# Seven half products for eight in part of the first FFN product, with copies moved to GpSimd: an attention and FFN kernel on one core

## The chip, the core and the metric

One core of a Trainium2 chip. Its engines are TensorE (PE: matmuls, and PEld: the weight loads beside them), VectorE (DVE), ScalarE (ACT), GpSimd (POOL) and SyncE (SP), each with its own queue of instructions, tied together by semaphores. The metric is the time of one execution on the device in microseconds (us); less is better.

## The reference

Eight batches of local and global attention (8 heads of 64, 512 local and 32 global tokens, a window of 32 tokens to either side), and then an FFN with a gelu over all 4352 tokens:

```python
s_g = scale * q_g @ k_all.T;  out_g = softmax(s_g) @ v_all        # 32 global queries see all
s_l = [scale * q_l @ k_g.T, scale * q_l @ k_l.T inside |i - j| <= 32]
out_l = softmax(s_l) @ [v_g, v_l]
x = concat(out_g, out_l) as (tokens, 512)
h = x @ w_in                     # (tokens, 512) x (512, 2048): the first FFN product
g = h * (1 / (1 + exp(-1.702 * h)))
out = g @ w_out                  # (tokens, 2048) x (2048, 512): the second
```

Inputs and output are float32; the kernel multiplies in bf16 and sums in float32.

## The kernel before, in words

The order of all instructions is written out by hand (`tc.manual_schedule()`): each engine gets its instructions in the order of the Python statements, and the Tile layer adds the semaphore waits and rotates the buffers of each pool.

The attention works on `Quad`s (four heads of one batch), two per batch, called `a` and `c`, each in its wide form `Wide`. Keys and queries are loaded by DMAs on POOL's queue (`load`, L81 and L82; `v` in `load_v`, L98 and L100), turned by transposes on DVE (`Tk`, L512; `Tq`, L316), and rearranged by small copies: `kcopy` (L504, 192 float32 a partition), `qcopy` (L507, 384 bf16) and the four parts of `ext` (L538, L540, L543, L545: the columns of the global queries and keys). `S` makes scores (L560), `X` the exponentials on ACT (L571), `M` multiplies them by the mask (L576, on DVE, and once per batch on POOL), `U` and `Gm` the products with `v` (L586, L597), `R` the reciprocal of the sums, with two transposes on DVE through the tiles `sT` and `rs` (L462 to L466), and `XL` the result (L471), which is the batch's `xL`, [128, 4, 512] in bf16: 512 channels in four blocks, 512 tokens.

The first FFN product of a batch is 16 calls of `h_step(i, fc)`: four matmuls of 512 columns (L615, one for each block of channels) into a PSUM bank `hp`, then one gelu on ACT (L620) into block `fc` of `gT`. Blocks are paired: pair `g` is the blocks 2g and 2g+1. The four `pbank` banks (`hp`, `ov`, `px` and others) rotate; the pairs of double banks from `spair` hold scores.

The second FFN product of batches 2 to 7 and of the 256 global rows (called batch 8) is written as seven half products for eight (`Pair`, L701 on): sums of quarters of `gT` (`g_sums`, on DVE, L696 and L699, in calls over groups of pairs), sums of the weights made once (`weight_sums`), seven products `mm(1)` to `mm(7)` of 256 columns (L726) into the banks `px` and `py`, and the combining steps `m3` (ACT), `z`, `zm`, `sub`, `add` (DVE) and `evict` (ACT) into `zz` and `ob`, which goes out by DMAs on SP's queue.

For batch i from 2 on the program alternates. First come the 16 steps of the first product, between which stand the transposes and copies of the next batch's `c` and of the batch after next's `a` (called `a2`), and the `g_sums` of the blocks that are ready:

```python
for fc in range(FC):
    h_step(i, fc)
    ...
    if i + 1 < B:
        c = nq[i + 1][1]
        if fc == 1:
            c.Tk(); c.Tq(); c.ext((3,))
        if fc in (3, 5, 7):
            c.ext(((3, 5, 7).index(fc),), on_act)
        if fc == 9 and i + 2 < B:
            a2 = quads_of(i + 2)[0]
            a2.T(); transpose_g(2 * i + 4, 2 * i + 6); a2.ext()
    if fc in (4, 8, 12):
        g_sums(i, fc // 2 - 2, fc // 2)
```

Then `phase_o(i)` interleaves the two `Pair`s of the second product, `p0` and `p1`, with the attention of batch i + 1, and at its end issues the loads of later batches (`loads_after`). After batch 7 the steps of the 256 global rows stand between the products of batch 7.

Of the kernel before, what the change touches and what calls it, by code (L numbers as in the profile page):

```python
# [12 lines left out]
F32 = mybir.dt.float32  # L13
# [3 lines left out]
ALU = mybir.AluOpType  # L17
# [3 lines left out]
def kernel(  # L21
# [90 lines left out]
    def on_act(out_, in_):  # L112
        nc.scalar.activation(out_, in_, AF.Copy)  # L113
# [166 lines left out]
    def pbank(name):  # L280
        return psP.tile([128, 512], F32, name=name, tag="p")


    def spair():
        return [psS.tile([128, 2, 512], F32, name="s4", tag="s%d" % i) for i in range(2)]
# [4 lines left out]
    class Quad:  # L290
        def __init__(self, Q):
            self.Q = Q
            self.b, self.u = divmod(Q, 2)
            if self.u == 0:
                xL[self.b] = att.tile([128, NKC, Sl], BF16, name="xL", bufs=2)
            self.x = xL[self.b]
            self.v = v_view(self.b, 5 if self.b else 4)[:, self.u]
            self.qt = qtiles[Q % 4]
            self.q = self.qt.bitcast(BF16).rearrange("p t (r e) -> p t r e", e=2)
            self.qg = qgT[:, Q, :32].bitcast(BF16).rearrange("p (s e) -> p s e", e=2)  # L300
            self.kg = kgT[:, Q].bitcast(BF16).rearrange("p (s e) -> p s e", e=2)
            self.E = [None, None]
            self.bk = {}
            self.st = {}
            self.pt = None
            self.gr = 1
# [297 lines left out]
            self.Gm()  # L604

    gTs, ops = {}, {}

    def width(i):
        return TB if i < B else B * Sg
# [3 lines left out]
    def h_mm(i, fc, hp, kcs):  # L613
        for kc in kcs:
            nc.tensor.matmul(hp[:, : width(i)], lhsT=w_in_c[:, fc // 4, kc, fc % 4 // 2, :, fc % 2],  # L615
                             rhs=(xL[i] if i < B else xG)[:, kc, :],
                             start=(kc == 0), stop=(kc == NKC - 1))

    def gelu(out_, in_):
        nc.scalar.activation(out_, in_, AF.Gelu_apprx_sigmoid)  # L620
# [15 lines left out]
    def h_act(i, fc, hp):  # L636
        n = width(i)
        gelu(gTs[i][:, fc, :n], hp[:, :n])

    def h_step(i, fc):  # L640
        if fc == 0:
            gTs[i] = (moe.tile([128, FC, TB], BF16, name="gT") if i < B else
                      early.bitcast(BF16).rearrange("p a b -> p (a b)").rearrange("p (f t) -> p f t", f=FC))
        hp = pbank("hp")
        h_mm(i, fc, hp, range(NKC))
        h_act(i, fc, hp)

    def o_mm(i, st, out=True, part=range(4)):
        tci, f4 = divmod(st, 4)
        first = (i, tci) not in ops  # L650
        if first:
            ops[i, tci] = pbank("op")
        op = ops[i, tci]
        for fc in [4 * f4 + n for n in part]:
            nc.tensor.matmul(op, lhsT=gTs[i][:, fc, tci * 128 : tci * 128 + 128],  # L655
                             rhs=w_out_sb[:, fc, :], start=(first and fc == 4 * f4), stop=(fc == FC - 1))
        if f4 == 3 and 3 in part and out:
            o_out(i, tci, op)

    HT = TB // 2  # L660
    HM = d_model // 2
    w_out_c = w_out_sb.rearrange("p (g e) m -> p g e m", e=2)
    b11, b12, b21, b22 = (w_out_c[:, :, e, h * HM : h * HM + HM] for e in range(2) for h in range(2))
    wsum = [wts.tile([128, FC // 2, HM], BF16, name="wsum%d" % k) if k in (0, 3, 4) else (b12, b21)[k - 1]
# [36 lines left out]
    class Pair:  # L701
# [5 lines left out]
        def mm(self, *ks):  # L707
            i, tt = self.i, self.tt
            n = width(i) // 2
            a11, a12, a21, a22 = parts_of(i)  # L710
            s = sums[i]
            for k in ks:
                lv, rv, where = {
                    1: (s[0], wsum[0], 2), 2: (s[2][:, :, n : 2 * n], b11, 1), 3: (a11, wsum[1], 0),
                    4: (a22, wsum[2], 1), 5: (s[2], b22, 0), 6: (s[1], wsum[3], 3), 7: (s[3], wsum[4], 2),
                }[k]
                if self.apart:
                    out_ = self.banks[where][:, :HM]
                else:
                    if k == 3:  # L720
                        self.x = self.banks[0] if self.banks else pbank("px")
                    if k == 1:
                        self.y = self.banks[1] if self.banks else pbank("py")
                    out_ = (self.y if where > 1 else self.x)[:, where % 2 * HM : where % 2 * HM + HM]
                for g in range(FC // 2):
                    nc.tensor.matmul(out_, lhsT=lv[:, g, tt * 128 : tt * 128 + 128], rhs=rv[:, g, :],  # L726
                                     start=(g == 0 and k in ((1, 3, 4, 6) if self.apart else (1, 3))), stop=(g == FC // 2 - 1 and k in (2, 5, 6, 7)),
                                     skip_group_check=True)

        def m3(self, eng="act"):  # L730
            self.zz = moe.tile([128, 2, HM], F32, name="zz")
            if eng == "act":
                on_act(self.zz[:, 0], self.x[:, :HM])
            else:
                nc.vector.tensor_copy(self.zz[:, 0], self.x[:, :HM])

        def z(self):
            nc.vector.tensor_add(self.zz[:, 0], self.zz[:, 0], self.x[:, HM:])

        def zm(self):  # L740
            nc.vector.tensor_add(self.zz[:, 1], self.zz[:, 0], self.y[:, :HM])
# [5 lines left out]
        def sub(self):  # L747
            nc.vector.tensor_sub(self.zz, self.zz, self.x.rearrange("p (h m) -> p h m", h=2))  # L748

        def add(self):  # L750
            nc.vector.tensor_add(self.ob[:, 0:4:3], self.zz, self.y.rearrange("p (h m) -> p h m", h=2))
# [104 lines left out]
    c.G()  # L856
    for fc in range(4, FC):
        h_step(0, fc)
    def osteps(i, *sts):
        for tci, f4 in sts:  # L860
            o_mm(i, 4 * tci + f4)
# [105 lines left out]
    def quads_of(n):  # L967
        if n < B and n not in nq:
            nq[n] = (Wide(2 * n), Wide(2 * n + 1))
        return nq.get(n, (None, None))  # L970
# [44 lines left out]
    def phase_o(i):  # L1015
        b = i + 1
        a, c = nq[b]
        a2, c2 = quads_of(b + 1)
        p0, p1 = Pair(i, 0), Pair(i, 1)
        exp_table()  # L1020
        a.UG()
        c.S(0)
        a.R()
        g_sums(i, 7, 8, (0,))
        a.XL(0)
        g_sums(i, 7, 8, (1, 2))
        a.XL(1)
        g_sums(i, 7, 8, (3,))
        p0.mm(3, 4, 1)
        c.X(0)  # L1030
        p0.m3()
        p0.z()
        a.G()
        c.M(0)
        c.S(1)
        c.X(1)
        p0.mm(6)
        p0.zm()
        c.M(1)
        p0.mm(5, 2)  # L1040
        p0.sub()
        p0.evict()
        p0.mm(7)
        p0.add()
        p0.store()
        if a2:
            c.UG()
            c.R()
            a2.S(0)
            a2.X(0)  # L1050
            a2.M(0, nc.gpsimd)
            loads_after(i + 1)
        else:
            pt = spair()
            c.U(0, bank(pt, 0))
            c.U(1, bank(pt, 2))
            c.U(2, bank(pt, 3))
            c.Gm(bank(pt, 1))
            c.R()
        c.XL(0)  # L1060
        if a2:
            c.XL(1)
            c.G()
        p1.mm(3, 4)
        p1.m3()
        p1.z()
        if not a2:
            c.XL(1)
            c.G()
        p1.mm(1, 6)  # L1070
        p1.zm()
        if a2:
            a2.S(1)
            a2.X(1)
        p1.mm(5, 2)
        p1.sub()
        p1.evict()
        gelu_table()
        p1.mm(7)
        p1.add()  # L1080
        if a2:
            a2.M(1)
        p1.store()

    for i in range(1, B):
        if i > 1:
            for fc in range(FC):
                h_step(i, fc)
                if i == 2 and fc == 0:
                    weight_sums(1, 2)  # L1090
# [3 lines that stand above are left out]
                        c.Tk()  # L1094
                        c.Tq()
                        c.ext((3,))
# [4 lines that stand above are left out]
                        a2.T()  # L1101
                        transpose_g(2 * i + 4, 2 * i + 6)
                        a2.ext()
                if fc in (4, 8, 12):
                    g_sums(i, fc // 2 - 2, fc // 2)
                if fc == 13:
                    g_sums(i, 6, 7)
        if i == 1:
            phase_o1()
        elif i + 1 < B:  # L1110
            phase_o(i)
# [88 lines left out]
```

## Time and profile before

| what | value |
|---|---|
| time, median of 3 runs | 286.68 us (286.36 to 286.75) |
| the profiled execution's own time | 286.51 us |
| its span in the trace | 284.5 us |
| PE busy | 279.1 us, 98% of the span, 3727 matmuls |
| DVE busy | 205.2 us, 72%, 498 instructions |
| ACT busy | 183.7 us, 65%, 293 |
| POOL busy | 95.2 us, 33%, 142 |
| granted TensorE clock | 1.0 |

PE's busy share alone does not say that PE is the limit, because matmuls overlap each other in the records; the chain of waits and the starts of successive matmuls do. The durations below are those of the one profiled execution. Times in the timelines count from the start of the span, and 2.0 us of the execution's own time lie outside it.

### The profile page before, as it was taken

How to read it: one execution, taken by the hardware profiler on the slowest of the kernel's cores; microseconds unless marked ns; L12 is line 12 of the kernel's file. 1: busy time of each engine (PE TensorE's matmuls, PEld its weight loads, DVE VectorE, ACT ScalarE, POOL GpSimd, SP SyncE). 2: the span in 40 equal slices, each digit the busy share in tenths (PEclk: the TensorE clock that was granted, in tenths of full speed). 3: DMA queues.
4: the chain of work that ended last, by engine and by line, in shares of the span. 5: the costliest groups of instructions: out<-in, count | busy, mean ns of one | idle time of the engine just before them, and what ended most of it. 6: DMA issues, size and time to landing. Idle time of an engine off the chain costs nothing.

```text
span 284.5 us, 8846 instructions
## 1 busy us (share of the span) xinstructions
PE 279.1 (98%) x3727; PEld 179.6 (63%) x3727; DVE 205.2 (72%) x498; ACT 183.7 (65%) x293; POOL 95.2 (33%) x142
## 2 busy tenths in 40 slices
PE   8999999999999999999999999999999999999994
PEld 7554445444554488647884588547874588448884
DVE  7670378995689998679957997779867697363452
ACT  4857568567778783878468764877568760873331
POOL 8974551857855002930077003900040000000001
PEclk9999999999999999999999999999999999999999
DMA  7999996999999702792039803970022003200213
GB/s 207 156 196 210 204 155 93 155 215 143 171 192 143 146 2 68 81 194 52 22 65 160 149 3 78 93 73 5 20 67 66 2 2 77 74 0 2 74 38 113
DMA packets 59351, 28.23 MB, mean 99 GB/s; under 512 B 47472, under 2 KB 49776, under 8 KB 59312
## 3 DMA queue, kind: packets, MB, share of 16 engines
q0 software_dynamic: 51760, 17.83, 55.3%
q1 hardware_dynamic: 7120, 9.18, 11.7%
q8 instruction: 29, 0.48, 0.7%
q10 hardware_dynamic: 432, 0.66, 0.7%
q14 instruction: 10, 0.08, 0.1%
HBM read 36.31 MB, written 8.91 MB: 159 GB/s over the span
## 4 chain that ended last, share of the span: by engine, by line
PE 94%; DVE 2%; DMA 1%; ACT 1%; SPq 0%; issue 0%; DVEq 0%
PE hp L615 38%; PE px L726 13%; PE op L655 10%; PE py L726 9%; PE x L726 6%; PE s L560 6%; PE ov L586 5%; PE s L615 3%; DMA early<-in_q_l_dram 1%; DVE xL L471 1%; PE og L597 1%; PE s L357 1%; ACT e L388 1%; PE ov L438 1%; PE s L340 1%; ACT e L385 0%
## 5 line engine op out<-in xcount | busy, mean ns | idle before, releaser
L615 PE MATMUL hp<-xL,w_in_sb 128*128 128x512 bf16 x480 | 105.4, 379 | 0.2 <-DVE xL L471 0.2
L615 PEld LDWEIGHTS <-w_in_sb 128*128 128x128 bf16 x576 | 56.1, 98 | 60.1 <-issue 0.4
L620 ACT ACTIVATE gT<-hp 128x512 bf16<-128x512 f32 x120 | 70.0, 596 | 25.1 <-PE hp L615 23.6
L571 ACT ACTIVATE e<-s 128x1016 bf16<-128x1016 f32 (+1 forms) x56 | 53.3, 1003 | 24.0 <-PE s L560 24.0
L726 PEld LDWEIGHTS <-gs 128*128 128x128 bf16 x480 | 46.3, 98 | 6.4
L699 DVE TENSOR_TENSOR gs<-gT 128x512 bf16<-128x512 bf16 (+1 forms) x90 | 30.3, 363 | 17.5 <-ACT gT L620 17.3
L576 POOL TENSOR_TENSOR e<-e,mask 128x1760 bf16<-128x1760 bf16 x4 | 13.3, 3320 | 83.4 <-ACT e L571 83.4
L98 POOL DMA_DIRECT2D v<-in_v_l_dram x40 | 31.1, 780 | 13.7 <-PE og L597 4.4
L726 PE MATMUL py<-wsum,gs 128*128 128x256 bf16 x240 | 30.3, 273 | 0.0
L655 PE MATMUL op<-w_out_sb,gT 128*128 128x512 bf16 x128 | 29.5, 380 | 0.0
L576 DVE TENSOR_TENSOR e<-e,mask 128x1712 bf16<-128x1712 bf16 (+1 forms) x24 | 25.1, 1048 | 3.7 <-ACT e L571 3.7
L512 DVE STREAM_TRANSPOSE kT<-rk 128x512 f32<-128x512 f32 x14 | 14.6, 1042 | 16.8 <-DMA rk<-in_k_l_dram 16.8
L759 POOL DMA_DIRECT2D out_dram<-ob x2 | 1.2, 597 | 68.2 <-ACT ob L113 68.0
L655 PEld LDWEIGHTS <-gT 128*128 128x128 bf16 x128 | 11.8, 98 | 14.0
L726 PEld LDWEIGHTS <-gT 128*128 128x128 bf16 x192 | 18.0, 98 | 2.9
L726 PE MATMUL px<-w_out_sb,gT 128*128 128x256 bf16 x160 | 19.2, 273 | 0.0
L726 PE MATMUL px<-w_out_sb,gs 128*128 128x256 bf16 x160 | 19.1, 273 | 0.0
L471 DVE TENSOR_TENSOR xL<-ov,rs 128x512 bf16<-128x512 f32 x27 | 17.9, 685 | 1.1 <-DVE rs L466 0.5
L696 DVE TENSOR_TENSOR gs<-gT 128x1024 bf16<-128x1024 bf16 (+1 forms) x30 | 17.3, 577 | 0.0
L560 PEld LDWEIGHTS <-kT 32*128 32x128 bf16 x672 | 12.5, 93 | 6.9 <-issue 4.9
L113 ACT ACTIVATE ob<-px 128x512 f32<-128x512 f32 x10 | 6.0, 599 | 15.2 <-DVE zz L748 15.2
L560 PE MATMUL s<-q,kT 32*128 32x160 bf16 (+1 forms) x448 | 14.7, 246 | 0.0
(153 smaller groups left out, 361.5 us busy)
## 6 DMA issues: line engine op xcount, KB each, us to landing
out_dram<-ob SPq DMA_DIRECT2D x128, 64.0 KB, 2.1
rq<-in_q_l_dram POOLq DMA_DIRECT2D x5, 512.0 KB, 8.5
rk<-in_k_l_dram POOLq DMA_DIRECT2D x5, 512.0 KB, 10.4
v<-in_v_l_dram POOLq DMA_DIRECT2D x24, 96.0 KB, 5.0
w_in_sb<-in_moe_w_in_dram POOLq DMA_DIRECT2D x8, 256.0 KB, 9.0
w_out_sb<-in_moe_w_out_dram POOLq DMA_DIRECT2D x4, 512.0 KB, 10.7
rk<-in_k_l_dram POOLq DMA_DIRECT2D x5, 256.0 KB, 7.2
rq<-in_q_l_dram POOLq DMA_DIRECT2D x5, 256.0 KB, 6.5
```

The source lines that it names most:

```text
L98: nc.gpsimd.dma_start(out=vt[0:n, hs, c, :D], in_=vs[FIRST[c] : FIRST[c] + n, hs])
L471: nc.vector.tensor_mul(self.x[:, 2 * self.u + h, :], self.st[1 + h], self.st["rs"])
L512: nc.vector.transpose(flat[:, 0:Sl].rearrange("p (r t) -> p t r", t=16), loaded[self.b][0][:, self.u].bitcast(F32))
L560: nc.tensor.matmul(bank(self.ps, j)[:, at : at + n], lhsT=self.k[p, KEYS[c] : KEYS[c] + 128, e], rhs=qs[p, :, :, e], start=(e == 0), stop= ...
L571: nc.scalar.activation(self.E[rnd][:, 2 * i : 2 * i + 2, :n], self.ps[i][:, :, :n], AF.Exp, scale=scale)
L576: eng.tensor_mul(e, e, mask[:, rnd : rnd + 1, :n].to_broadcast([128, 4, n]))
L615: nc.tensor.matmul(hp[:, : width(i)], lhsT=w_in_c[:, fc // 4, kc, fc % 4 // 2, :, fc % 2], rhs=(xL[i] if i < B else xG)[:, kc, :], start=( ...
L620: nc.scalar.activation(out_, in_, AF.Gelu_apprx_sigmoid)
L655: nc.tensor.matmul(op, lhsT=gTs[i][:, fc, tci * 128 : tci * 128 + 128], rhs=w_out_sb[:, fc, :], start=(first and fc == 4 * f4), stop=(fc = ...
L696: nc.vector.tensor_tensor(sums[i][2][:, g, :n], t[:, g, 0, :n], t[:, g, 1, :n], ALU.add)
L699: nc.vector.tensor_tensor(sums[i][k][:, g, : n // 2], x[:, g], y[:, g], op)
L726: nc.tensor.matmul(out_, lhsT=lv[:, g, tt * 128 : tt * 128 + 128], rhs=rv[:, g, :], start=(g == 0 and k in ((1, 3, 4, 6) if self.apart els ...
```

## The change

In batches 3 to 7 a new function `h_some` takes the place of the loop over `h_step`. It makes pair 1 (blocks 2 and 3), and in batch 7 also pairs 4 and 5 together, by seven products of half size in each dimension: `HPair`, which for each pair makes 7 x 2 matmuls of 256 columns in place of 2 x 4 of 512. The sums of the weights that these need are made once, on DVE in batch 0 (`h_weight_sums`, 5 for each pair, into the tile `early`); the sums of halves of `xL` are made on DVE in `phase_o` of the batch before (`x_sums`), into the tiles of `sT` and `rs` and a new tile `xs`. The double banks of `spair` take the products, and a tile of `ob`'s pool holds `zz`. `inner` and `outer` are the gelus of the pair, one from PSUM and one from `zz`.

In `h_some`, `kcopy`, `qcopy` and one part of `ext` of `c` and all of `a2`'s copies go to POOL (`nc.gpsimd.tensor_copy`) from DVE; three parts of `c`'s `ext` stay on ACT. The order of the transposes, of the copies and of the `g_sums` among the steps is new too. Batch 2 keeps the old loop.

```diff
+    w_h = {g: [w_in_c[:, g // 2, 2 * k : 2 * k + 2, g % 2, :, e] for e in range(2) for k in range(2)]
+           for g in (1, 4, 5)}
+    w_s = early.bitcast(BF16)...                      # 15 sums of [128, 2, 128]
+    def h_weight_sums(g):
+        w11, w12, w21, w22 = w_h[g]
+        for t, x, y, op in zip(wh[g], (w11, w21, w11, w21, w12), (w22, w22, w12, w11, w22),
+                               (ALU.add, ALU.add, ALU.add, ALU.subtract, ALU.subtract)):
+            nc.vector.tensor_tensor(t, x, y, op)
+    def x_sums(i):
+        ...
+        for o, x, y, op in zip(xs["d"], (x11, x12, x21), (x22, x22, x11), (ALU.add, ALU.subtract, ALU.subtract)):
+            nc.vector.tensor_tensor(o, x, y, op)      # 512 each
+        nc.vector.tensor_tensor(xs["s"], t[:, :, :HT], t[:, :, HT:], ALU.add)   # 1024
+    class HPair:
+        ...
+        def mm(self, *ks):
+            for k in ks:
+                for u, g in enumerate(self.gs):
+                    lv, rv, t, h = {
+                        1: (wh[g][0], xs["d"][0], self.y, 0), 2: (wh[g][1], xs["r"][0], self.x, 1),
+                        3: (w_h[g][0], xs["d"][1], self.x, 0), 4: (w_h[g][3], xs["d"][2], self.x, 1),
+                        5: (wh[g][2], xs["r"][1], self.x, 0), 6: (wh[g][3], xs["s"][:, 0:2], self.y, 1),
+                        7: (wh[g][4], xs["s"][:, 2:4], self.y, 0),
+                    }[k]
+                    for kc in range(2):
+                        nc.tensor.matmul(t[:, u, h * HT : h * HT + HT], lhsT=lv[:, kc], rhs=rv[:, kc, :], ...)
+        def m3(self):
+            on_act(self.zz[:, :, 0], self.x[:, :, :HT])
+        def z(self):
+            nc.vector.tensor_add(self.zz[:, :, 0], self.zz[:, :, 0], self.x[:, :, HT:])
+        def zm(self):
+            nc.vector.tensor_add(self.zz[:, :, 1], self.zz[:, :, 0], self.y[:, :, :HT])
+        def sub(self):
+            nc.vector.tensor_sub(self.zz, self.zz, self.x4)
+        def add(self):
+            nc.vector.tensor_add(self.zz, self.zz, self.y4)
+        def inner(self):
+            gelu(self.out[:, :, 1:3], self.x4)
+        def outer(self):
+            gelu(self.out[:, :, 0:4:3], self.zz)
...
     for fc in range(4, FC):
         h_step(0, fc)
+        if fc == 4:
+            h_weight_sums(1)
+        if fc == 12:
+            h_weight_sums(4)
+            h_weight_sums(5)
...
         p1.mm(1, 6)
         p1.zm()
+        x_sums(i + 1)
...
+    def h_some(i):
+        c = nq[i + 1][1] if i + 1 < B else None
+        a2 = quads_of(i + 2)[0] if i + 2 < B else None
+        pool = nc.gpsimd.tensor_copy
+        ...
+        for fc in range(2):
+            h_mm(i, fc, hps[fc], range(NKC))
+        p = HPair(i, 1)
+        p.mm(3, 4); p.m3()
+        for fc in range(2):
+            h_act(i, fc, hps[fc])
+        if c:
+            c.Tk(False); c.kcopy(pool)
+        p.z(); p.mm(1, 6); p.zm()
+        if c:
+            c.Tq(False); c.qcopy(pool); c.ext((3,), pool)
+        if a2:
+            a2.Tk(False); a2.kcopy(pool)
+        h_step(i, 4)
+        if c:
+            c.ext((0,), on_act)
+        h_step(i, 5)
+        p.mm(5, 2); p.sub(); p.inner(); p.mm(7); p.add()
+        h_step(i, 6)
+        p.outer()
+        if a2:
+            a2.Tq(False); transpose_g(2 * i + 4, 2 * i + 6); a2.qcopy(pool); a2.ext(copy=pool)
+        g_sums(i, 0, 2)
+        h_step(i, 7)
+        if c:
+            c.ext((1,), on_act)
+        g_sums(i, 2, 4)
+        if c:
+            for fc in range(8, 12):
+                h_step(i, fc)
+                if fc == 9:
+                    c.ext((2,), on_act)
+            g_sums(i, 4, 6)
+            h_step(i, 12); h_step(i, 13)
+        else:
+            p = HPair(i, 4, 5)
+            p.mm(3, 4); p.m3(); p.z(); p.mm(1, 6); p.zm()
+            h_step(i, 12)
+            p.mm(5, 2); p.sub(); p.inner(); p.mm(7); p.add()
+            h_step(i, 13)
+            p.outer()
+            g_sums(i, 4, 6)
+        g_sums(i, 6, 7)
+        h_step(i, 14); h_step(i, 15)
+
     for i in range(1, B):
-        if i > 1:
+        if i > 2:
+            h_some(i)
+        elif i > 1:
```

(Statements of one line each in the program are joined by semicolons here.)

More of the change, by code (lines that the diff above doesn't have):

```diff
@@ L606 @@
     gTs, ops = {}, {}
+    HT = TB // 2
+    HM = d_model // 2
     def width(i):
@@ L646, in h_step @@
         h_act(i, fc, hp)
+    w_h = {g: [w_in_c[:, g // 2, 2 * k : 2 * k + 2, g % 2, :, e] for e in range(2) for k in range(2)]
+           for g in (1, 4, 5)}
+    w_s = early.bitcast(BF16).rearrange("p a b -> p (a b)")[:, : 5 * 3 * 256].rearrange(
+        "p (k u c m) -> p k u c m", k=5, u=3, c=2)
+    wh = {g: [w_s[:, k, u] for k in range(5)] for u, g in enumerate(w_h)}
+    def h_weight_sums(g):
[3 more added lines that the diff above has]
+            nc.vector.tensor_tensor(t, x, y, op)
@@ new lines @@
+    xs = {}
+    def x_sums(i):
+        t = xL[i]
+        x11, x12, x21, x22 = (t[:, 2 * k : 2 * k + 2, h * HT : h * HT + HT] for k in range(2) for h in range(2))
+        r1 = att.tile([128, 16, 32], F32, name="sT", bufs=1).rearrange("p a b -> p (a b)").bitcast(BF16)
+        r2 = att.tile([128, 512], F32, name="rs", bufs=1).bitcast(BF16)
+        xs["d"] = [r.rearrange("p (k t) -> p k t", k=2) for r in (
+            r1[:, : 2 * HT], r1[:, 2 * HT :], moe.tile([128, 2 * HT], BF16, name="xs"))]
+        xs["s"] = r2.rearrange("p (k t) -> p k t", k=NKC)
+        for o, x, y, op in zip(xs["d"], (x11, x12, x21), (x22, x22, x11), (ALU.add, ALU.subtract, ALU.subtract)):
+            nc.vector.tensor_tensor(o, x, y, op)
+        nc.vector.tensor_tensor(xs["s"], t[:, :, :HT], t[:, :, HT:], ALU.add)
+        xs["r"] = (x11, x22)
@@ new lines, with __init__ @@
+    class HPair:
+        def __init__(self, i, *gs):
+            self.i, self.gs = i, gs
+            self.n = len(gs)
+            x, y = spair()
+            self.x, self.y = x[:, : self.n], y[:, : self.n]
+            self.x4, self.y4 = (t.rearrange("p u (h t) -> p u h t", h=2) for t in (self.x, self.y))
+            self.zz = moe.tile([128, 4, HM], F32, name="ob", bufs=3).rearrange(
+                "p (u h) t -> p u h t", u=2)[:, : self.n]
+            self.out = gTs[i][:, 2 * gs[0] : 2 * gs[0] + 2 * self.n, :].rearrange(
+                "p (u e) (h t) -> p u (e h) t", e=2, h=2)
+        def mm(self, *ks):
[8 more added lines that the diff above has]
+                    for kc in range(2):
+                        nc.tensor.matmul(t[:, u, h * HT : h * HT + HT], lhsT=lv[:, kc], rhs=rv[:, kc, :],
+                                         start=(kc == 0 and k in (1, 3)), stop=(kc == 1 and k in (2, 5, 6, 7)),
+                                         skip_group_check=True)
+        def m3(self):
[12 more added lines that the diff above has]
+            gelu(self.out[:, :, 0:4:3], self.zz)
@@ L658, in o_mm @@
             o_out(i, tci, op)
-    HT = TB // 2
-    HM = d_model // 2
     w_out_c = w_out_sb.rearrange("p (g e) m -> p g e m", e=2)
@@ L1083, in phase_o @@
         p1.store()
+    def h_some(i):
+        c = nq[i + 1][1] if i + 1 < B else None
+        a2 = quads_of(i + 2)[0] if i + 2 < B else None
+        pool = nc.gpsimd.tensor_copy
+        gTs[i] = moe.tile([128, FC, TB], BF16, name="gT")
+        hps = [pbank("hp"), pbank("hp")]
+        for fc in range(2):
+            h_mm(i, fc, hps[fc], range(NKC))
+        p = HPair(i, 1)
+        p.mm(3, 4)
+        p.m3()
+        for fc in range(2):
+            h_act(i, fc, hps[fc])
+        if c:
+            c.Tk(False)
+            c.kcopy(pool)
+        p.z()
+        p.mm(1, 6)
+        p.zm()
+        if c:
+            c.Tq(False)
+            c.qcopy(pool)
+            c.ext((3,), pool)
+        if a2:
+            a2.Tk(False)
+            a2.kcopy(pool)
+        h_step(i, 4)
+        if c:
+            c.ext((0,), on_act)
+        h_step(i, 5)
+        p.mm(5, 2)
+        p.sub()
+        p.inner()
+        p.mm(7)
+        p.add()
+        h_step(i, 6)
+        p.outer()
+        if a2:
+            a2.Tq(False)
+            transpose_g(2 * i + 4, 2 * i + 6)
+            a2.qcopy(pool)
+            a2.ext(copy=pool)
+        g_sums(i, 0, 2)
[13 more added lines that the diff above has]
+            p = HPair(i, 4, 5)
+            p.mm(3, 4)
+            p.m3()
+            p.z()
+            p.mm(1, 6)
+            p.zm()
+            h_step(i, 12)
+            p.mm(5, 2)
+            p.sub()
+            p.inner()
+            p.mm(7)
+            p.add()
+            h_step(i, 13)
+            p.outer()
+            g_sums(i, 4, 6)
+        g_sums(i, 6, 7)
+        h_step(i, 14)
+        h_step(i, 15)
     for i in range(1, B):
-        if i > 1:
+        if i > 2:
+            h_some(i)
+        elif i > 1:
             for fc in range(FC):
```

## The prediction

> **What bounds the kernel now.** I read the chain of waits first, in sum, then in order of time.
>
> ```profile
> PE 94%; DVE 2%; DMA 1%; ACT 1%; SPq 0%; issue 0%; DVEq 0%
> ```
> ```profile
> 210.67 0.87 PE py L726 x8
> 211.54 13.81 PE hp L615 x64
> ...
> 240.89 0.87 PE py L726 x8
> 241.76 14.25 PE hp L615 x68
> 256.01 0.87 PE x L726 x8
> 257.32 0.87 PE x L726 x8
> ```
>
> TensorE sets the end. Each piece starts where the one before it stops: from 85 us on nothing holds PE up, so every matmul saved shortens the run and every wait put before one lengthens it. Prices: 64 matmuls of 512 columns in 13.81 us are 215.8 ns each; 8 of 256 columns in 0.87 us are 109.3 ns. Between the last two pieces stand 4 matmuls of 256 columns with weights from `w_in_sb`, in 1.31 - 0.87 = 0.44 us: the same price with the strided weights that the new products use too.
>
> Then the timelines of DVE, ACT and POOL, for what room lies beside that chain. DVE and ACT where batch 7 begins (start, duration, idle before and its releaser):
>
> ```profile
> 240.93 0.69 DVE L748 TENSOR_TENSOR zz<-zz,px 128x512 f32<-128x512 f32 x1 [0.92 <-PE px L726]
> 241.80 0.69 DVE L751 TENSOR_TENSOR ob<-zz,py 128x512 f32<-128x512 f32 x1 [0.19 <-PE py L726]
> 245.88 0.76 DVE L699 TENSOR_TENSOR gs<-gT 128x512 bf16<-128x512 bf16 x2 [3.39 <-ACT gT L620]
> 246.56 0.69 DVE L696 TENSOR_TENSOR gs<-gT 128x1024 bf16<-128x1024 bf16 x1
> 247.16 0.42 DVE L699 TENSOR_TENSOR gs<-gT 128x512 bf16<-128x512 bf16 x1
> 249.34 0.76 DVE L699 TENSOR_TENSOR gs<-gT 128x512 bf16<-128x512 bf16 x2 [1.76 <-ACT gT L620]
> ```
> ```profile
> 242.26 1.28 ACT L620 ACT_TABLE_LOAD   x1
> 243.56 0.20 ACT L620 ACTIVATE spot<-spot 128x1 f32<-128x1 f32 x1
> 243.67 2.18 ACT L620 ACTIVATE gT<-hp 128x512 bf16<-128x512 f32 x4
> ```
>
> A gelu of 512 takes 0.60 us and one follows the other by 0.52. One `g_sums` call of two groups holds DVE for 1.61 us (0.34 for each op of 512, 0.60 for the one of 1024).
>
> **PE, the gain.** A pair of blocks was 8 x 215.8 = 1.726 us and becomes 14 x 109.3 = 1.530: 0.196 less. Seven pairs: **-1.37 us**. The new matmuls wait neither for a bank nor for `x_sums` where they start; what they wait for later is the question.
>
> **Work with cover.** The 15 weight sums, at 0.3 to 0.4 us (rows of 256 and 512), take 4.5 to 6 us of DVE in batch 0, ahead of the first `kT` transpose of batch 1. Cover:
>
> ```profile
> 33.31 1.04 DVE L512 STREAM_TRANSPOSE kT<-rk 128x512 f32<-128x512 f32 x1 [12.23 <-DMA rk<-in_k_l_dram]
> ```
>
> Zero; without that wait they would cost what exceeds it. `x_sums` is 3 x 0.34 + 0.60 = 1.62 us, put between `zm` and `sub` of `p1`, where DVE idles 1.99 us in batches 2 to 5: zero. In batch 6 there is 0.92, so `sub`, the eviction and the table load behind it slip 0.6 us; ACT takes that up in batch 7 before product 5 (below). Two gelus become m3 (0.38), inner and outer (0.60 each), 0.4 us more, where ACT idles 0.27 us at each of the later steps.
>
> Batches 3 to 6, from PE's start of the batch: z waits for `add`, the mask and `kT` on DVE and is done at 3.1 us, zm at 3.4; PE comes to product 5 at 4.33 and product 7 at 4.76. No wait. outer ends at 7.5, and with the copies gone the last `g_sums` ends at 13.95 (14.62 now), before U(0) is through at 14.2. POOL's queue holds the loads of `v` until 4.9 (153.42 less 148.54), then `rq`, which waits for Tq as now (4.0), then `rk` (to 6.3); the nine copies follow. c's three are wanted by c.S(0) at 15.0, a2's six by a2.S(0) about 23. POOL copy prices:
>
> ```profile
> L225 POOL COPY mask<-band 96x192 bf16<-96x192 bf16 x2 | 1.1, 534 | 0.0
> ...
> L225 POOL COPY mask<-band 128x72 bf16<-128x72 bf16 x1 | 0.3, 297 | 0.0
> ```
>
> That is 2 ns per element over 0.16 us: 0.5 (192), 0.65 (256), 0.9 (384), so some 2.1 us for c and 3.2 for a2, done by 11.6. Zero, unless they hold up DVE (rival A).
>
> **Batch 7, the loss.** Here 4,5 is a second, double pair, and DVE stands in its way. From PE's start of the batch, with nothing waiting: steps 0, 1 and pair 1's products 3, 4, 1, 6 to 2.60; steps 4, 5 to 4.33; 5, 2, 7 to 4.98; steps 6, 7 to 6.71; the double pair's 3, 4, 1, 6 (0.437 each) to 8.46; step 12 to 9.32; then its product 5, whose first matmul waits, in the built program, for its z on DVE. When is z done?
> - ACT: table at about 2.5, m3, gelus 0, 1, 4, 5 to 5.0. inner waits for `sub` (product 2 ends 4.76, `sub` 0.69): 5.55. gelu 6 at 6.07, outer 6.59 to 7.19, gelu 7 to 7.71.
> - DVE: `g_sums` 0 to 2 wait for outer: 7.23 to 8.84. `g_sums` 2 to 4: to 10.45. Both stand ahead of z in DVE's queue. z of 512 (0.69): 11.14.
>
> PE can go on at 11.2, not 9.32: **+1.88 us**. zm (11.75) is done before product 7 is reached. Behind it `sub` and `add` of 1024 (0.41 for 256, 0.69 for 512: an estimate of 1.24 each), inner and outer (1.02, row of 1024) put outer's end at 15.9 and gelu 14's at 16.4; the px product that follows step 0 of the last batch wants gelu 14's block at 16.31: **+0.16**. The sums of the last groups arrive in time for product 1.
>
> Sum: -1.37 + 1.88 + 0.16 = +0.67. On the profiled run's own 286.51 that is 287.18; the median of the runs, 286.68, lies 0.17 above it, so I forecast **287.4 us**. Error: gaps between DVE instructions and the waits on stores ahead of m3 and z add 0 to 0.3; outer 0.5 earlier or later moves it by that much.
>
> **Rival A: copies and sums exclude each other.** On POOL, the copies of batches 3 to 5 run beside `g_sums` on DVE. No row shows a DVE sum beside a POOL copy. The nearest, DVE beside a POOL load, points both ways:
>
> ```profile
> 183.57 0.80 POOL L98 DMA_DIRECT2D v<-in_v_l_dram  x1
> ```
> ```profile
> 183.75 0.26 DVE L507 COPY qc<-q 128x384 bf16<-128x384 bf16 x1
> 183.93 0.47 DVE L545 COPY kT<-kgT 128x256 bf16<-128x256 bf16 x1
> 184.16 0.76 DVE L699 TENSOR_TENSOR gs<-gT 128x512 bf16<-128x512 bf16 x2
> ```
>
> The DVE copy (0.22 elsewhere) ends with POOL's instruction; the sums after it run through the next load undisturbed. If a copy and a sum took turns, some 3.2 us of a2's copies would lie in the time of the sums in batches 3 and 4, and 2.4 in 5. DVE has 1.4 us to spare: 0.55 of waits for gelus between its sums, and 0.85 from 13.95 until R has to start so that `sT` frees the bank of px, wanted at 15.53. Lost: 1.8 + 1.8 + 1.0 = 4.6, hence 292.0 at the far end; nothing, 287.4, if DVE keeps its turn through a run of sums. It decides from 1.4 us of delay per batch. I take half, 289.7.
>
> [...]
>
> **Rival B: the gain arrives.** If z were done by about 10.1 instead of 11.14, the hold-up in batch 7 would be under 0.8 us and the run faster by over 0.57; with none, 286.68 - 1.37 = 285.3. For it: all else is covered, and PE's saving is plain arithmetic. Against it: outer cannot come before its chain of gelus on ACT, and 3.2 us of sums stand ahead of z.
>
> **How the numbers follow.** Forecast (one hold-up, in batch 7): 0.55, between 286.4 and 287.9. Rival A: 0.35. Rival B: 0.10. About 0.2%, 0.57 us, is what a measurement of this kernel tells from no change: slower begins at 287.25, just under the forecast, so of its 0.55 I give 0.27 to no change and 0.28 to slower. Faster 0.10, same 0.27, slower 0.63. The range, 286.2 to 291.2, leaves out most of B and the outer part of A. The forecast's own is 286.4 to 287.9.
>
> **What would show it.** Right: in batch 7, about 1.9 us of PE idle before product 5 of pair 4,5, released by DVE's z, and PE's chain of batches 3 to 6 unbroken, with 13.62 us for the first product of each. Wrong by A: `g_sums` records stretched to the end of POOL copies, and a PE wait for `sT` or DVE at the px products. Wrong by B: `g_sums` 0 to 4 over by 9 us of batch 7. The 14 matmuls at more than 109 ns would break the gain, an idle DVE before 33 us gone would break the cover of the weight sums.

## The result, and the profile after

| | before | after |
|---|---|---|
| time, median | 286.57 us (286.36 to 286.79, 8 runs) | 288.66 us (287.35 to 289.49, 8 runs) |
| ratio after / before | | 1.0066 (1.0044 to 1.0088) |
| the profiled execution's own time | 286.51 us | 287.64 us |
| its span | 284.5 us | 285.9 us |
| DVE busy | 205.2 us | 231.9 us |
| POOL busy | 95.2 us | 108.0 us |

The changed kernel is slower, by 0.4 to 0.9%. Its eight runs fall into two groups: three at 287.35 to 287.70 us with a granted TensorE clock of 1.0 over the span, and five at 288.55 to 289.49 us with 0.993 or 0.994. The profiled execution belongs to the first group; a profile of the second is in the first experiment.

In the chain of waits PE's share falls from 94 to 91%. The first line of the list of PE's waits (which line waited for what: us in total, times, longest):

```profile
PE s L699 <- DVE ob L707: 2.0, 1, 2.0
```

L699 is the products of `HPair`, L707 its `z`. It is the longest wait in PE's list, and the kernel before has none like it. The PE and DVE timelines of batch 7 (start, duration, idle before and its releaser) show where it stands:

```profile
249.75 1.03 PE L617 MATMUL hp<-xL,w_in_sb 128*128 128x512 bf16 x4
252.74 1.03 PE L699 MATMUL s<-xL,early 128*128 128x256 bf16 x8 [1.96 <-DVE ob L707]
...
254.05 2.75 PE L617 MATMUL hp<-xL,w_in_sb 128*128 128x512 bf16 x12
```
```profile
248.79 0.76 DVE L773 TENSOR_TENSOR gs<-gT 128x512 bf16<-128x512 bf16 x2 [0.70 <-ACT gT L622]
249.47 0.68 DVE L770 TENSOR_TENSOR gs<-gT 128x1024 bf16<-128x1024 bf16 x1
250.07 1.09 DVE L773 TENSOR_TENSOR gs<-gT 128x512 bf16<-128x512 bf16 x3
251.08 0.68 DVE L770 TENSOR_TENSOR gs<-gT 128x1024 bf16<-128x1024 bf16 x1
251.68 0.41 DVE L773 TENSOR_TENSOR gs<-gT 128x512 bf16<-128x512 bf16 x1
252.01 0.68 DVE L707 TENSOR_TENSOR ob<-ob,s 128x512 f32<-128x512 f32 x1
```

PE is through step 12 at 250.78 and stands until 252.74. DVE is never idle from 248.79 on: it makes the two `g_sums` calls (0 to 4) that stand ahead of z in its queue, in 3.22 us, and only then z.

Counted from start to start the hold-up is longer than its row says. The row of the four matmuls ahead of it lasts 1.03 us, four spacings of 215.8 ns only 0.86: the record of a last matmul outlasts its spacing by about 0.16 us. The next matmul could have started at 250.61, 2.13 us before it did. Behind the wait PE runs at full pace: the 12 matmuls of products 5, 2 and 7 take 254.05 - 252.74 = 1.31 us, 12 x 0.109.

Batches 3 to 6 are the other half of the picture. The chain of batch 3 in order of time:

```profile
117.47 1.73 PE hp L617 x8
119.20 0.87 PE s L699 x8
120.07 1.73 PE hp L617 x8
121.80 0.66 PE s L699 x6
122.45 8.63 PE hp L617 x40
131.09 1.20 PE ov L586 x56
```

From 117.47 to 131.09 are 13.62 us without a break, where the kernel before took 13.81. From batch start to batch start the four batches take 31.32, 31.35, 31.30 and 30.02 us, before 31.58, 31.50, 31.50 and 30.22. So the profiled execution gains 0.81 us up to batch 7. The chain of batch 7:

```profile
241.46 1.73 PE hp L617 x8
...
257.24 1.11 PE x L800 x8
```

The stretch from its start to the first half product of its second product (L800, before L726) goes from 14.25 to 15.78 us, 1.53 more. That half product itself, which waits for gelu 14, goes from 0.87 to 1.11, 0.24 more.

### The profile page after: what moved, and what is told of

The parts are those of the page before. It is cut to its first block, busy times and chain, and to the rows that moved or that the text cites. A ratio compares the mean times of both kernels' runs of the same rounds, so it can differ in the third digit from the quotient of the medians.

```text
span 285.9 us, 9019 instructions
## 1 busy us (share of the span) xinstructions
PE 278.1 (97%) x3769; PEld 183.5 (64%) x3769; DVE 231.9 (81%) x527; ACT 181.9 (64%) x297; POOL 108.0 (38%) x172
## 4 chain that ended last, share of the span: by engine, by line
PE 91%; DVE 3%; DMA 2%; POOL 1%; ACT 1%; issue 1%; DVEq 0%; POOLq 0%
PE hp L617 33%; PE px L800 13%; PE op L731 10%; PE py L800 9%; PE x L800 7%; PE s L560 6%; PE ov L586 5%; PE s L699 3%; PE s L617 2%; DMA rq<-in_q_l_dram 2%; DVE xL L471 1%; DVE gs L773 1%; PE og L597 1%; PE ov L438 1%; ACT e L385 0%
## 5 line engine op out<-in xcount | busy, mean ns | idle before, releaser
L617 PE MATMUL hp<-xL,w_in_sb 128*128 128x512 bf16 x424 | 95.3, 379 | 0.2 <-DVE xL L471 0.2
L617 PEld LDWEIGHTS <-w_in_sb 128*128 128x128 bf16 x520 | 50.6, 98 | 50.9 <-issue 0.4
L622 ACT ACTIVATE gT<-hp 128x512 bf16<-128x512 f32 x106 | 61.4, 600 | 17.1 <-PE hp L617 16.6
L800 PEld LDWEIGHTS <-gs 128*128 128x128 bf16 x480 | 46.2, 98 | 6.5
L773 DVE TENSOR_TENSOR gs<-gT 128x512 bf16<-128x512 bf16 (+1 forms) x90 | 31.6, 385 | 4.1 <-ACT gT L622 4.1
L800 PE MATMUL py<-wsum,gs 128*128 128x256 bf16 x240 | 30.3, 273 | 0.0
L800 PEld LDWEIGHTS <-gT 128*128 128x128 bf16 x192 | 17.9, 98 | 3.3 <-ACT gT L622 0.4
L800 PE MATMUL px<-w_out_sb,gT 128*128 128x256 bf16 x160 | 19.2, 273 | 0.0
L800 PE MATMUL px<-w_out_sb,gs 128*128 128x256 bf16 x160 | 19.1, 273 | 0.0
L622 ACT ACTIVATE gT<-s 128x1024 bf16<-128x1024 f32 (+1 forms) x10 | 8.0, 810 | 12.0 <-DVE ob L713 7.4
```

The source lines that it names most:

```text
L773: nc.vector.tensor_tensor(sums[i][k][:, g, : n // 2], x[:, g], y[:, g], op)
```

## The experiments

Theory H: the hold-up in batch 7 makes the loss. Rival I: the lower clock of some runs has nothing to do with it. Rival A is that of the prediction.

**The changed kernel again.** No edit; it was run beside the next three on one chip.

> The changed kernel itself, run again beside the others on one chip. Both theories: two groups of runs as before, one near 287.5 us at a granted clock of 1.0 and one 1 to 2 us above it at a mean clock of 0.993 or 0.994. What is wanted is how often the second comes, and whether a profile shows where in the span the clock is low.

288.18 us (287.29 to 289.16, 6 runs), ratio 1.0052 (1.0033 to 1.0071): four runs at 287.29 to 288.19 with clock 0.999 or 1.0, two at 288.61 and 289.16 with 0.994. Its profiled execution was one of the two. The PE timeline shows the same hold-up, with matmuls behind it that take longer:

```profile
252.27 1.16 PE L699 MATMUL s<-xL,early 128*128 128x256 bf16 x8 [1.97 <-DVE ob L707]
...
254.08 3.93 PE L617 MATMUL hp<-xL,w_in_sb 128*128 128x512 bf16 x12
```

These 12 matmuls took 2.75 us in the other profile. Stretches of 0.25 us, with the granted clock in the third column from the end:

```profile
253.00:253.25 0.25, 0.25 (x4) 0.18 (x3) 0.01 (x1) 0.00 (x0) 0.00 (x0) 0.59 0.00 0
...
256.25:256.50 0.25, 0.25 (x2) 0.12 (x1) 0.00 (x0) 0.25 (x1) 0.00 (x0) 0.59 0.00 0
```

In between it is 0.50. A mean of 0.59 over 0.25 us is a clock of 0.50 for 0.205 us of it, so the clock is halved at 253.04 and restored at 256.46: 3.41 us at half speed, 2.74 us after PE fell idle.

**The sums later.** In batch 7, `g_sums(i, 2, 4)` goes from ahead of pair 4,5 to behind its `add`.

```diff
-        g_sums(i, 2, 4)
         if c:
+            g_sums(i, 2, 4)
...
             p.add()
+            g_sums(i, 2, 4)
             h_step(i, 13)
```

> The changed kernel with one edit: in batch 7 the sums of groups 2 and 3 on DVE stand behind add of the double pair instead of ahead of its z. Theory H (the hold-up makes the loss, and the low clock follows from the hold-up): z of the double pair ends 1.61 us earlier, TensorE waits 0.3 us before product 5 instead of 1.96, so the runs at full clock fall from 287.6 to about 286.0, and there are no runs at 0.993: median 286.0, 0.2% under the kernel before. Rival I (the low clock has nothing to do with the hold-up): the same 1.6 us are won, but more than half of the runs still show 0.993 and lie 1 to 2 us above the others.

286.01 us (285.63 to 286.56, 12 runs), ratio 0.9978 (0.9969 to 0.9988). The wait before product 5:

```profile
250.65 1.03 PE L699 MATMUL s<-xL,early 128*128 128x256 bf16 x8 [0.38 <-DVE ob L707]
```

1.6 us less wait, and no run under 0.997. In its profile, itself at 0.997, the clock falls only in the last fortieth of the span (0.62 from 282.0 to 283.9 us), not behind the wait. One line of order turns the change from a loss into a gain: H holds.

**Pair 1 alone.** Batch 7 gets no pair 4,5; its blocks 8 to 13 are made by plain steps.

```diff
-            p = HPair(i, 4, 5)
-            ...
+        for fc in range(8, 12):
+            h_step(i, fc)
+            if c and fc == 9:
+                c.ext((2,), on_act)
+        g_sums(i, 4, 6)
```

> The changed kernel without the double pair 4,5 in batch 7 (its four blocks are ordinary steps again); pair 1 stays in batches 3 to 7. Theory H: no hold-up, five pairs at 0.196 us saved = 0.98 us, so 285.6 to 285.9 us with every run at clock 1.0. Rival I: the same time at full clock, with runs at 0.993 among them. Were the copies on GpSimd what costs, this kernel would stay above 286.6.

286.08 us (285.35 to 286.41, 9 runs), ratio 0.9967 (0.9951 to 0.9982), every clock at 0.999 or 1.0, no wait for z. Five pairs at 0.196 are 0.98 us. The ratio makes the gain 0.95 us (0.5 to 1.4), the medians only 0.57, less than the 0.75 to 1.05 that were expected. One batch of its profile, batch 3, took 31.56 us (see "no wait at all").

**The kernel before, held up.** No half products; DVE repeats a `g_sums` call ahead of the last sums, so that a half product of batch 7's second product has to wait about as long as product 5 did.

```diff
+    for _ in range(3):
+        g_sums(B - 1, 0, 2)
+    g_sums(B - 1, 0, 2, (0, 1))
     g_sums(B - 1, 7, 8)
```

> The kernel before with a hold-up put in and nothing else: ahead of the last sums of batch 7, DVE makes the sums of groups 0 and 1 over again, three times in full and half a time more (the same values into the same tiles), about 5.5 us of DVE. TensorE then waits once, about 1.9 us, before the last matmul of a product 1 of batch 7. Theory H: +1.9 us at full clock (288.5), and part of the runs at a mean clock near 0.993 and another 1 to 2 us longer. Rival I: +1.9 us and all runs at 1.0.

288.88 us (288.55 to 291.38, 6 runs), ratio 1.0095 (1.0065 to 1.0124).

```profile
260.91 1.05 PE L726 MATMUL x<-wsum,gs 128*128 128x256 bf16 x8 [2.13 <-DVE gs L699]
```

Four runs at 288.55 to 288.93 with clock 0.999 or 1.0; two at 290.35 and 291.38 with 0.994. The lower clock comes without anything of the change but its wait, so rival I falls.

**No wait at all.** As "the sums later", and of `g_sums(0, 2)` only half stands ahead of z; the sums of groups 6 and 7 are made together, behind the steps.

```diff
-        g_sums(i, 0, 2)
+        g_sums(i, 0, 2, (0, 1, 2, 3) if c else (0, 1))
...
             g_sums(i, 2, 4)
+            g_sums(i, 0, 2, (2, 3))
...
-    g_sums(B - 1, 7, 8)
+    g_sums(B - 1, 6, 8, (0,))
+    g_sums(B - 1, 6, 8, (1, 2, 3))
```

> The kernel of e1_sums_later with the rest of the wait taken out: in batch 7 only two of the four sums of groups 0 and 1 stay ahead of z of the double pair, the other two follow its add, and the sums of groups 6 and 7 are made together, the one that product 1 needs first. Theory H: TensorE's 0.38 us before product 5 go, the saving of 1.37 us stands whole but for 0.2 us behind gelu 14: 285.6 us, granted clock above 0.996 in every run. Rival J (the double pair pushes its wait on to the products of the last batch, because DVE has 10 us of work in the stretch): TensorE waits for a sum there instead, and the time stays at 286.0.

286.08 us (285.43 to 286.51, 12 runs), ratio 0.9975 (0.9962 to 0.9988), no run under 0.997. The wait before product 5 is gone, and yet the kernel isn't faster than "the sums later". Its profile shows two reasons. One is rival J's: in the second product of batch 7 a product 1 waits for a sum, and the matmuls from the first half product on take 0.24 us more than in "the sums later".

```profile
259.28 0.39 PE L800 MATMUL x<-wsum,gs 128*128 128x256 bf16 x2 [0.15 <-DVE gs L773]
```

The other is that two of the four batches take 31.56 and 31.57 us, not 31.3. The first sums of batch 3 on DVE, in the changed kernel and, second, here:

```profile
125.39 1.26 DVE L773 TENSOR_TENSOR gs<-gT 128x512 bf16<-128x512 bf16 x2
```
```profile
125.41 1.98 DVE L773 TENSOR_TENSOR gs<-gT 128x512 bf16<-128x512 bf16 x2
```

Undisturbed, the two take 0.76 (batch 7, above). Up to 127.1 the last four of a2's copies run on POOL (L538 to L545). Here they go ahead and take 1.3 us together, to 127.11, and the two sums end behind the last of them, at 127.39. In the changed kernel sums and copies alternate (the two sums end at 126.21 and 126.65, L538 and L540 at 126.36 and 126.83), the copies take 2.0 us (one of them, L538, 0.56 in place of 0.28), and the sums are through 0.25 us earlier. Here `sT` follows at 132.42 and px at 133.17, 0.2 us later than it could. So rival A is real and has a price of about 0.2 us a batch where the copies come first. Which comes first changed between these two kernels though nothing in batch 3 differs between them ("pair 1 alone" has the 1.98 in batch 3, which took 31.56 us, while its batch 4 took 31.32); what decides it was not tried.

**The copies back on DVE.** As "no wait at all", with the copies on the engine that had them before.

```diff
-        pool = nc.gpsimd.tensor_copy
+        pool = nc.vector.tensor_copy
```

> The kernel of e4_no_wait with all of the copies of keys and queries that went to GpSimd back on DVE. By the exclusion of copies and sums (theory L): nine copies of 0.17 to 0.27 us, 1.9 us a batch, come back to DVE, about as much as the sums lost beside the copies on GpSimd (1.5 to 2 us a batch); DVE's chain ends within 0.5 us of where it did, no wait on TensorE, time within 0.2 us of e4_no_wait. Rival M (GpSimd takes real work off DVE): DVE's last sums of a batch end 1.5 us later, the px products wait for sT by some 0.5 us in batches 3 to 5, and the kernel is 1 to 1.5 us slower than e4_no_wait.

289.33 us (289.22 to 289.63, 5 runs), ratio 1.0089 (1.0068 to 1.0111): 3.25 us over "no wait at all", at clocks of 0.998 to 1.0. Batches 3 to 5 take 32.3 to 32.5 us each. In batch 4, which starts at 149.52, px comes at

```profile
166.23 1.91 PE L800 MATMUL px<-w_out_sb,gT 128*128 128x256 bf16 x16
```

16.71 us in, against 15.65 in batch 3 of the changed kernel. DVE then has the work of the half products and the copies in one queue, and its last sums and `sT` are late. Three batches take 1.0 to 1.2 us more than 31.3, where the stretched sums cost "no wait at all" 0.25 in each of two; batch 6 takes 0.4 more. Theory L, within 0.2 us, falls, and rival M holds at twice the size expected. In this order of the program the move to GpSimd is what makes room for the half products; with the copies on DVE no other order was tried.

**A shorter hold-up.** The kernel before with three repeated sums less.

```diff
+    for _ in range(2):
+        g_sums(B - 1, 0, 2)
+    g_sums(B - 1, 0, 2, (0, 1, 2))
     g_sums(B - 1, 7, 8)
```

> The kernel before with a shorter hold-up than in e3_before_held: 4.5 us of repeated sums on DVE, which holds TensorE for about 1.1 us once. If the clock falls when TensorE is idle through part of a stretch that is counted from its own start, the chance grows with the length of the hold-up: here few or no runs at 0.994, time 287.7. If any hold-up of this place does it, a third to a half of the runs lie near 0.994 and at 289.

287.69 us (287.19 to 288.93, 12 runs), ratio 1.0037 (1.0023 to 1.0051). PE waits twice, 0.52 and 0.20 us, and the product ends 1.07 us later than its eight matmuls need; 0.37% of 286.57 is 1.06. No run is under 0.997.

**A longer hold-up.** The same with four calls and two sums.

```diff
+    for _ in range(4):
+        g_sums(B - 1, 0, 2)
+    g_sums(B - 1, 0, 2, (0, 2))
     g_sums(B - 1, 7, 8)
```

> The kernel before with a longer hold-up: 7.4 us of repeated sums, which holds TensorE for about 4.0 us once. If the chance of the low clock grows with the length of the hold-up, all runs are at 0.994 or lower, 290.6 us for the hold-up alone and 292 to 292.5 with the clock; if it does not, a third to a half of them.

293.03 us (291.86 to 294.32, 6 runs), ratio 1.0222 (1.0194 to 1.025). All six runs have a lower clock: 0.994 twice (291.86, 292.94), 0.988 four times (292.91 to 294.32). The profile is one of the latter; the wait, and stretches with the clock as above:

```profile
263.52 1.89 PE L726 MATMUL x<-wsum,gs 128*128 128x256 bf16 x8 [3.74 <-DVE gs L699]
```
```profile
262.50:262.75 0.25, 0.00 (x0) 0.00 (x0) 0.25 (x2) 0.00 (x0) 0.00 (x0) 0.58 0.00 0
262.75:269.25 6.50, 5.73 (x27) 4.08 (x28) 3.83 (x14) 0.77 (x2) 0.00 (x0) 0.50 0.01 3
269.25:269.50 0.25, 0.25 (x4) 0.23 (x2) 0.12 (x1) 0.00 (x0) 0.00 (x0) 0.77 0.00 0
```

Half speed begins at 262.54, while PE still stands, and ends at 269.37: 6.83 us, twice the 3.41 of the first experiment. The time lies above the 292 to 292.5 that were expected with a lower clock.

**The copies alone.** The kernel before, in whose loop the same copies go to GpSimd for i over 2; no half products.

```diff
                     if fc == 1:
-                        c.Tk()
-                        c.Tq()
-                        c.ext((3,))
+                        cp = nc.gpsimd.tensor_copy if i > 2 else nc.vector.tensor_copy
+                        c.Tk(cp)
+                        c.Tq(cp)
+                        c.ext((3,), cp)
...
-                        a2.T()
+                        a2.Tk(cp)
+                        a2.Tq(cp)
                         transpose_g(2 * i + 4, 2 * i + 6)
-                        a2.ext()
+                        a2.ext(copy=cp)
```

> The kernel before with nothing changed but the engine of the copies: in batches 3 to 6 kcopy, qcopy and ext part 3 of c and all copies of a2 go to GpSimd from DVE; no half products. Theory H (the copies as such cost and give nothing that PE sees; the loss of the change is the hold-up in batch 7): 286.4 to 286.9, ratio within 0.2% of 1, no PE wait before a product of the first FFN part, periods of 31.5 us as in the kernel before. Rival A (copies on GpSimd and sums on DVE exclude each other, and PE waits for the late sT or gs): some periods of 31.7 to 32.5 us, 287.2 or more. If the copies were a gain by themselves, periods would be under 31.5, and the 0.2 us that each batch saves in the changed kernel would not be the half products' alone.

286.61 us (286.01 to 286.99, 12 runs), ratio 0.9999 (0.999 to 1.0008). From its chain of waits, the first products of batches 3 and 4:

```profile
117.36 13.81 PE hp L615 x64
...
148.86 13.81 PE hp L615 x64
```

31.50 us a batch, as before. DVE's first sums beside the copies took 1.00 to 1.12 us in place of 0.76, and PE saw nothing of it. By themselves, in the old order, the copies cost and give nothing that these runs show; the 0.2 us a batch in the changed kernel are the half products'.

## Why the prediction was right, and what it missed

The forecast of slower held, and its mechanism, the hold-up in batch 7, is shown by the runs. The size holds for the runs at full clock alone. The median of 288.66 lies above the forecast's own 286.4 to 287.9, and within the whole range, 286.2 to 291.2, only because that was widened for rival A, which cost PE nothing in the changed kernel: that part is luck. The steps of the forecast, in us:

| step | predicted | measured |
|---|---|---|
| gain of batches 3 to 6 | 0.78 (4 pairs at 0.196) | 0.81 |
| batch 3's first product, from PE's start | 13.62, unbroken | 13.62, unbroken |
| weight sums in batch 0 | 4.5 to 6, hidden | 5.08, and DVE idles 5.46 behind them |
| batch 7: outer's end, from PE's start | 7.19 | 7.30 |
| `g_sums` 0 to 4 | 3.22 | 3.22 |
| batch 7: PE ready for product 5 | 9.32 | 9.32 |
| z of pair 4,5 done | 11.14 | 11.23 |
| hold-up | 1.88 | 1.96 by the wait row, 2.12 from start to start |
| gelu 14 ahead of the second product | 0.16 | 0.24 |

In the profile of full clock the parts add up to -0.81 - 0.59 (three pairs in batch 7) + 2.12 + 0.24 = +0.96, where the sum gave +0.67. The 0.16 between the last two numbers of the hold-up was left out of the sum: it took PE's start of the batch from the chain, whose pieces begin where the record before ends, 0.16 us after the first matmul starts, and set DVE's and ACT's times against that. Start to start, this wait takes 0.16 us more than its row shows. Seven runs of the changed kernel at clocks of 0.999 and up have a median of 287.70, 1.05 to 1.13 over the kernel before; that is the forecast, 287.4, with an error of 0.3, the size that it gave itself.

What it missed is in the other seven of the fourteen runs. Their median is 288.99, 1.3 us higher, and the runs with hold-ups of several lengths tie that to the wait:

| wait of PE | kernels | runs with a clock of 0.994 or less |
|---|---|---|
| none put in | kernel before, beside all others | 1 of 68 |
| 0 to 0.4 us | sums later, pair 1 alone, no wait at all, copies back, copies alone | 0 of 50 |
| 0.52 and 0.20 us | shorter hold-up | 0 of 12 |
| 1.96 to 2.13 us | changed kernel (14 runs), kernel before held up | 9 of 20 |
| 3.74 us | longer hold-up | 6 of 6 |

It isn't the chip: on the one that ran the first four experiments, 4 of 12 runs with a wait of 2 us had the lower clock and 0 of 21 without; on the next, 6 of 6 with the longest wait and 0 of 29 with shorter ones. So a term is missing in the sum: a hold-up of 2 us costs PE its length and, in about half the executions (9 of 20 here), another 1.3 us at a mean clock of 0.993 or 0.994 (0.50 for 3.41 us in the one profile of such a run). The sum was made as if a wait cost only itself. Over many runs that term is worth about 0.65 us, half of 1.3; with it and the 0.16 the sum would have been 288.2, not 287.4. The median of all fourteen runs is 288.37.

Rival B stated the condition under which the change would pay, a hold-up under 0.8 us. "The sums later" made it 0.38 and was 0.22% faster, which is what 1.37 less 0.38 + 0.16 and 0.24 leaves: 0.59 us, or 0.21%.

Rival A named an effect that the rows show (two sums of 0.76 us take 1.26 to 1.98 beside copies) and priced it too high. Its copies were costed at 2.1 us for c and 3.2 for a2 from the rows of the strided mask copies; they take 1.1 (0.36, 0.52 and 0.41 one behind the other) and 2.0 undisturbed. The first six sums of a batch, 2.37 us in batch 7, took 3.37 in batch 3 of the changed kernel, a delay of 1.0 without a wait of PE, and 3.59, a delay of 1.2, in "no wait at all", with 0.2 lost; the 1.4 us from which it was to decide were too many by some 0.3. The clearest case is one that the prediction put at nothing, the `x_sums`. In batch 2 they run beside the mask multiplication on POOL, in batch 6 POOL is idle. First two of the sums in each of these batches, then POOL in batch 2:

```profile
114.56 2.08 DVE L673 TENSOR_TENSOR sT<-xL 128x512 bf16<-128x512 bf16 x2
...
239.63 0.73 DVE L673 TENSOR_TENSOR sT<-xL 128x512 bf16<-128x512 bf16 x2
```
```profile
112.69 3.32 POOL L576 TENSOR_TENSOR e<-e,mask 128x1760 bf16<-128x1760 bf16 x1 [20.41 <-ACT e L571]
```

The first sum ends at 116.30, only after POOL's instruction has ended at 116.01; it takes 1.74 us, the second 0.41. So `x_sums` takes 3.0 us, more than the 1.99 of idle time that it was to fill. In batch 3 z is done 3.66 us in, not 3.1, and zm 4.18, not 3.4. Product 5, which waits for z, comes at 4.33, and product 7, which waits for zm, at 4.76. The cover held with about 0.6 us to spare for each, not 1.2 and 1.4. These rows show a sum on DVE that started 1.87 us after a POOL instruction and ended 0.29 us after it; what decides which instructions hold each other up no run here shows.

Open: one run of the kernel before, of 68, had a clock of 0.992 and 288.12 us without any hold-up. Batch 0's blocks start 0.54 us later in the profile of after than in that of before; over the experiments' profiles that start lies between 20.8 and 22.1 us in both kinds of kernel, so it is not put down to the change. It is in the spans of the two profiles, which differ by 1.4 us, and not in the +0.96.

## What to carry to other kernels

Before an engine is given a new step that TensorE will wait for, list what stands ahead of it in that engine's queue at that moment: here 3.2 us of sums that nobody wanted yet made a gain of 1.4 us into a loss, and moving one call of them behind the step gave a kernel faster than both (286.01 against 286.65). Price a wait of TensorE in an otherwise full stretch by its length from start to start, not by its row (0.16 us more here), and, at 2 us, by an even chance (9 of 20 runs here) of another 1.3 us at a lower clock. Work that GpSimd does beside sums on VectorE was not free of itself here: two sums of 0.76 us took 1.26 to 1.98 beside copies. Look at the rows of the pair together, stretched against unstretched, before a move to GpSimd is put at nothing.

## What the runs showed of the hardware that was not expected

Of the 20 runs with a wait of 1.96 to 2.13 us in the midst of dense matmuls, 9 had a mean granted clock of 0.993 or 0.994; of the 6 with a wait of 3.74 us all had 0.988 or 0.994. Of each sort one run with the lower clock was profiled, and in both profiles the clock fell to 0.50: for 3.41 us in the first experiment's, with a wait of 1.97, and for 6.83 in the longer hold-up's. It fell 2.74 us after PE went idle in the one, and 2.76 in the other, where PE was still idle.

How much idle time is enough, and why some executions of a kernel had the lower clock and others not, no run here shows. The counts are 0 of 12 with waits of 0.52 and 0.20 us, 9 of 20 at about 2 us and 6 of 6 at 3.74; hold-ups of lengths in between were not run.
